# A head that centres tokens without a diagonal, and a fourth token tile that is loaded, normalised and transposed on its own

## The chip, the cores and the metric

The kernel runs on one core of one Trainium2 chip. The metric is the device time of one execution in microseconds; lower is better. The engines are named by what they do: TensorE (PE in the profile; its weight loads are PEld), VectorE (DVE), ScalarE (ACT), GpSimd (POOL) and SyncE (SP, which here only issues DMAs).

## What is computed

Two branches over the same layer-normalised input are added to the input itself. x is 2048 tokens by 512 features in bfloat16.

```python
xn = (x - mean(x)) / sqrt(var(x) + 1e-5)            # per token
# branch A: a diagonal complex state space model (S5)
Lam_bar = exp(exp(log_dt) * Lam)                    # 512 complex states
B_bar   = ((Lam_bar - 1) / Lam)[:, None] * (B_re + 1j * B_im)
Bu      = xn @ B_bar.T                              # 2048 x 512, complex
h[t]    = Lam_bar * h[t - 1] + Bu[t]                # scan over the 2048 tokens
y       = 2 * real(h @ C.T) + xn * Dskip
# branch B: SwiGLU, 512 -> 1376 -> 512
z = (silu(xn @ w_gate) * (xn @ w_up)) @ w_down
out = x + y + z
```

## The kernel before

The 2048 tokens are cut into four chunks of 512 (`CW`), and each chunk into four tiles of 128 tokens (`TPC`). The 1376 columns of `w_gate` and `w_up` are cut into three groups, `fgroups`: columns 0 to 511, 512 to 1023 and the rest. Loops are written out at build time, and the order of the instructions on every engine and queue is the order in which the code emits them (`manual_schedule`). Work of VectorE that isn't urgent is kept in a list, `backlog`, and emitted between TensorE's stages by `pump`, which counts off estimated microseconds; that order is fixed at build time too. Every TensorE result goes to a PSUM bank from a pool of eight (`bank()`), so that a new result waits until the tile eight before it has been read by ScalarE or VectorE.

**Loads.** SyncE issues the loads one after the other: x of tile 0, half of gate group 0 (L119), x of tile 2 (L132), both halves of up group 0, x of tile 3 (L135), gate and up of groups 1 and 2 (L114), and x of tiles 4 to 7 (L144). ScalarE's queue issues x of tile 1 and the other half of gate group 0.

**The head.** Most of the kernel needs the normalised input with features on the partitions. For chunk 0 that would take statistics, normalisation and a transpose before TensorE could begin. So the first three tiles (`SW` = 3) go another way: they are only centred (mean subtracted), transposed by TensorE against the identity (`cT_mm`, L242) and copied out of PSUM into `xcT` (`cT_copy`, L254); the factor 1/std of a token is put in later, as a scale of the ScalarE instruction that reads the gate or up result (`sw_gate` L500, `sw_out` L515).

For tiles 0 and 1 the mean is subtracted inside TensorE: `raw_mm` transposes the raw tile into PSUM, and `cT_mean` (L250) adds a product of the constant `minus_mean` (-1/512 everywhere) with `diag`, the identity scaled per token with the token's sum. The sum of tile 0 is a VectorE reduction (L219), that of tile 1 a ScalarE instruction (L222), and `diag` is built by VectorE (L229). For tile 2 the mean is a ScalarE instruction (`mean_act`, L225), the subtraction a VectorE instruction (`center`, L232), and TensorE transposes the centred tile. `head_mm` (L492, as all of `sw_mm`) then multiplies these tiles with group 0 of gate (which = 0) and up (which = 1), over four blocks k of 128 features each.

**Tile 3 and the rest of chunk 0.** `ln_stats` (L185, L186), `ln_rstd` (L194 on VectorE, the power -1/2 at L195 on GpSimd) and `norm_dve` (L203) normalise the four tiles into `xn_c[0]`, which shares its memory with the centred tiles, and one DMA transpose (`xT_dma`, L262) brings all four into `xnT[:, 0]`. Tile 3 of SwiGLU's first products and the state space projection of chunk 0 (`bproj_tile`, L384) read it. Behind it in SyncE's queue are the two transposing loads of the projection's weights `BT` (L148).

In between stand small steps for the state space model: `prm_transpose` (a TensorE product L278 and a VectorE copy L279), `exp_pool` (L282, a power on GpSimd), `pad_last` (three GpSimd memsets), an iota on GpSimd (L744), `params_a` (L285, L287), and `params_sin` (L323 to L339, two ScalarE sines). `table_ops` builds tables of sines from VectorE steps (L298 to L307) and ScalarE sines (L311).

**SwiGLU of chunk 0.** The remaining pairs of group and tile follow in this order, with L769 for the pairs of group 2, whose gate and up share one bank:

```python
for gi, i in [(1, 0), (1, 1), (1, 2), (2, 0), (2, 1), (2, 2), (0, 3), (1, 3), (2, 3)]:
```

The products of gate and up are VectorE instructions (L523). Then come the projection of chunk 0 (32 matmuls over eight banks), the last, narrow block of SwiGLU (`gateup_last`, L542, read by L544 and L545), the projection of chunk 1, and SwiGLU, scan, and output of the chunks in turn (L459, L426, L598, L611). The output is accumulated in memory: x is copied to the output by DMAs of 256 rows (`edges`, L857) and results are added by accumulating DMAs.

Of the kernel before, what the change touches and what calls it, by code (L numbers as in the profile page):

```python
# [10 lines left out]
F32 = mybir.dt.float32  # L11
# [12 lines left out]
def kernel(  # L24
# [52 lines left out]
    def flat(ap3):  # L77
        return ap3.rearrange("p q j -> p (q j)")
# [33 lines left out]
    def load_w1(q, tiles, view, gi):  # L112
        a, b = fgroups[gi]
        q.dma_start(out=tiles[gi][:, :, :], in_=view[:, :, a * 128:F if gi == len(fgroups) - 1 else b * 128])  # L114
# [9 lines left out]
    minus_mean = const.tile([128, 128], BF16, name="minus_mean")  # L124
    nc.sync.dma_start(out=xall[:, 0, :], in_=x_v[:, 0, :])
    nc.vector.memset(xall[:, 1, 0:2], 0.0)
    nc.vector.memset(minus_mean[:], -1.0 / D)
    nc.scalar.dma_start(out=xall[:, 1, :], in_=x_v[:, 1, :])
    nc.scalar.preload_act_table_set("silu_and_others")
    load_w1_half(nc.sync, wg_g, wg_v, 0, 0, HK)  # L130
# [1 line left out]
    nc.sync.dma_start(out=xall[:, 2, :], in_=x_v[:, 2, :])  # L132
    load_w1_half(nc.sync, wu_g, wu_v, 0, 0, HK)
    load_w1_half(nc.sync, wu_g, wu_v, 0, HK, KD)
    nc.sync.dma_start(out=xall[:, 3, :], in_=x_v[:, 3, :])  # L135
    load_w1(nc.sync, wg_g, wg_v, 1)
    load_w1(nc.sync, wu_g, wu_v, 1)
    load_w1(nc.sync, wg_g, wg_v, 2)
    load_w1(nc.sync, wu_g, wu_v, 2)
    prm_rows = const.tile([128, 128], BF16, name="prm_rows")  # L140
# [40 lines left out]
    def by_k(ap):  # L181
        return ap.rearrange("p (k d) -> p k d", d=128)

    def ln_stats(n):
        nc.vector.bn_stats(out=stats[:, n, 0, :], in_=xall[:, n, :])  # L185
        nc.vector.bn_aggr(out=mv[:, n, :], in_=stats[:, n, 0, :])  # L186
# [6 lines left out]
    def ln_rstd(a, b):  # L193
        nc.vector.tensor_scalar(out=ve[:, a:b], in0=mv[:, a:b, 1], scalar1=EPS, scalar2=None, op0=ALU.add)  # L194
        nc.gpsimd.tensor_tensor(out=rstd[:, a:b], in0=ve[:, a:b], in1=neg_half[:, 0:b - a], op=ALU.pow)  # L195
# [15 lines left out]


    xcT, xc = CF[:, 0], CF[:, 1]
    xn_c[0] = flat(xc).rearrange("p (k i d) -> p k i d", k=KD, i=TPC)
    sums = const.tile([128, 2], F32, name="sums")
    diag = const.tile([128, 2, 128], BF16, name="diag")

    def sum_dve(i):
        nc.vector.tensor_reduce(out=sums[:, i:i + 1], in_=xall[:, i, :], axis=mybir.AxisListType.X, op=ALU.add)  # L219

    def sum_act(i):
        nc.scalar.activation(out=xnT[:, NCH - 1, 0, :], in_=xall[:, i, :], func=ACT.Copy, accum_out=sums[:, i:i + 1])  # L222

    def mean_act(i):
        nc.scalar.activation(out=xnT[:, NCH - 1, 0, :], in_=xall[:, i, :], func=ACT.Copy, scale=1.0 / D,  # L225
                             accum_out=mean2[:])

    def diag_dve(i):
        nc.vector.tensor_scalar(out=diag[:, i, :], in0=ident[:], scalar1=sums[:, i:i + 1], scalar2=None, op0=ALU.mult)  # L229

    def center(i, mean):
        nc.vector.tensor_scalar(out=xc[:, i, :], in0=xall[:, i, :], scalar1=mean, scalar2=None, op0=ALU.subtract)  # L232

    mean2 = const.tile([128, 1], F32, name="mean2")
    p2, p0, p1 = bank(), bank(), bank()
    held = [[None, None] for _ in range(TPC)]
    held[0][0], held[1][0], held[0][1], held[1][1], held[2][0] = (bank() for _ in range(5))
    warm = held[1][0]
    raw = [[p0, p1, held[2][0], held[1][1]], [p2, p2, held[0][1], held[0][1]]]

    def cT_mm(ps, src, k, first, stop):
        nc.tensor.matmul(ps[:, k * 128:(k + 1) * 128], lhsT=src[:, k * 128:(k + 1) * 128], rhs=ident[:], start=first,  # L242
                         stop=stop)

    def raw_mm(i):
        for k in range(KD):
            cT_mm(raw[i][k], xall[:, i, :], k, k == 0 or raw[i][k] is not raw[i][k - 1], False)

    def cT_mean(i, k0, k1):
        nc.tensor.matmul(raw[i][k0][:, k0 * 128:k1 * 128], lhsT=minus_mean[:],  # L250
                         rhs=diag[:, i:i + 1, :].to_broadcast([128, k1 - k0, 128]), start=False, stop=True)

    def cT_copy(copy, ps, i, k0=0, k1=KD):
        copy(out=xcT[:, k0:k1, i * 128:(i + 1) * 128], in_=by_k(ps[:, k0 * 128:k1 * 128]))  # L254

    seen = const.tile([128, 1], BF16, name="seen")

    def runs(ap):
        return ap.rearrange("p k (i t) -> p (k i) t", t=128)

    def xT_dma(c):
        nc.sync.dma_start_transpose(out=runs(xnT[:, c]), in_=xn_tile(c)[:].rearrange("p k i d -> p (k i d)"))  # L262
# [13 lines left out]
    def prm_transpose():  # L276
        pp = p1[:, 0:128]
        nc.tensor.matmul(pp, lhsT=prm_rows[:], rhs=ident[:], start=True, stop=True)  # L278
        V.tensor_copy(out=prm[:].rearrange("p t q -> p (t q)"), in_=pp[:, 0:3 * NQ])  # L279

    def exp_pool(out, in_):
        nc.gpsimd.tensor_tensor(out=out, in0=e_t[:], in1=in_, op=ALU.pow)  # L282
# [96 lines left out]
    def bproj_tile(c, part, q):  # L379
        if c not in u_tiles:  # L380
            u_tiles[c] = ssm.tile([128, 2, NQ, CW], BF16, name="u16", bufs=2)
        ps = bank()
        for k in range(KD):
            nc.tensor.matmul(ps[:], lhsT=BT[:, part, k, q * 128:(q + 1) * 128], rhs=xnT[:, c, k, :],  # L384
                             start=(k == 0), stop=(k == KD - 1))
        nc.scalar.copy(out=u_tiles[c][:, part, q, :], in_=ps[:])  # L386

    def rotation(src, dst, back):
# [88 lines left out]
            g, u = guT[:fs, lo:fi + 1, :], u_pair[c][:fs, 0:fi - lo + 1, :]  # L477
            products.append(lambda: V.tensor_tensor(out=g, in0=g, in1=u, op=ALU.mult))  # L478

    SW = TPC - 1  # L480
    gu_tile(0)
    g0 = flat(gu_tile(1)[:]).rearrange("p (f i d) -> p f i d", f=FT, i=TPC)

    def tokens(i, k):
        if i < SW:
            return xcT[:, k, i * 128:(i + 1) * 128]
        return xnT[:, 0, k, i * 128:(i + 1) * 128]

    def sw_mm(ps, groups, gi, i, k0=0, k1=KD):
        a, b = fgroups[gi]  # L490
# [44 lines left out]
    def gateup_last(c):  # L535
        gl = g_last[c % 2][:] if c else g0[:, FT - 1]
        u = up_p.tile([128, TPC, FR], BF16, name="ul", bufs=2)
        for h in range(0, TPC, 2):
            ps = bank()[:, 0:4 * FR].rearrange("p (i w f) -> p i w f", i=2, w=2)
            for i in range(2):  # L540
                for k in range(KD):
                    nc.tensor.matmul(ps[:, i], lhsT=xnT[:, c, k, (h + i) * 128:(h + i + 1) * 128],  # L542
                                     rhs=w_end[:, k, :, FL - FE:FL - FE + FR], start=(k == 0), stop=(k == KD - 1))
            nc.scalar.activation(out=gl[:, h:h + 2, 0:FR], in_=ps[:, :, 0, :], func=ACT.Silu)  # L544
            nc.scalar.copy(out=u[:, h:h + 2, :], in_=ps[:, :, 1, :])  # L545

        def product():
            V.tensor_tensor(out=gl[:, :, 0:FR], in0=gl[:, :, 0:FR], in1=u[:], op=ALU.mult)
            if c:
                nc.sync.dma_start_transpose(out=gu_tile(c)[:, FT - 1:FT, :].rearrange("p f (i t) -> p (f i) t", t=128),  # L550
                                            in_=gl.rearrange("p i d -> p (i d)"))
            else:
                g0_dma(fgroups[1][1], FT)
        products.append(product)
# [111 lines left out]
    def dummy(ps, n, cols):  # L666
        for _ in range(n):
            nc.tensor.matmul(ps[:, 0:cols], lhsT=one.to_broadcast([128, 128]), rhs=one.to_broadcast([128, cols]),  # L668
                             start=True, stop=True)
# [22 lines left out]
    def head_mm(which, i, k0=0, k1=KD):  # L692
        if held[i][which] is None:
            held[i][which] = bank()
        sw_mm(held[i][which], (G, U)[which], 0, i, k0, k1)

    dummy(warm, 4, CW)
    dummy(warm, 5, 128)
    V.tensor_copy(out=seen[:], in_=ident[:, 0:1])
    sum_dve(0)  # L700
    sum_act(1)
    diag_dve(0)
    raw_mm(0)
    raw_mm(1)
    dummy(warm, 2, 128)
    for k in range(KD):
        cT_mean(0, k, k + 1)
    diag_dve(1)
    for k in range(KD):
        cT_copy(nc.scalar.copy if k % 2 else V.tensor_copy, raw[0][k], 0, k, k + 1)  # L710
    cT_mean(1, 0, HK)
    head_mm(0, 0, 0, 1)
    cT_mean(1, HK, KD)
    cT_copy(V.tensor_copy, raw[1][0], 1, 0, HK)
    cT_copy(nc.scalar.copy, raw[1][HK], 1, HK, KD)
    head_mm(0, 0, 1, HK)
    head_mm(0, 1, 0, HK)
    for k in range(HK, KD):
        for i in range(2):
            head_mm(0, i, k, k + 1)  # L720
    ln_stats(1)
    mean_act(2)
    ln_rstd(1, 2)
    ln_stats_half(0, 0)
    center(2, mean2[:])
    ln_stats_half(0, 1)
    ln_rstd(0, 1)
    for i in range(2):
        head_mm(1, i, 0, HK)
    for k in range(KD):  # L730
        cT_mm(p1, xc[:, 2, :], k, k == 0, k == KD - 1)
    cT_copy(nc.scalar.copy, p1, 2)
    for i in range(2):
        head_mm(1, i, HK, KD)
    ln_stats(3)
    ln_rstd(3, 4)
    ln_stats(2)
    ln_rstd(2, 3)
    head_mm(0, 2)
    sw_gate(0, 0, held[0][0])  # L740
    prm_transpose()
    exp_pool(dt_t[:], ldt)
    pad_last()
    nc.gpsimd.iota(out=jidx[:], pattern=[[1, CW]], base=0, channel_multiplier=0,  # L744
                   allow_small_or_imprecise_dtypes=True)
    sw_out(0, 0, None, held[0][1])
    head_mm(1, 2)
    for n in range(TPC):
        norm_dve(n)
    xT_dma(0)  # L750
    params_a()
    load_bt(0)
    load_bt(1)
    sw_out(0, 1, *held[1])
# [97 lines left out]
    gateup_chunk(1)  # L852
    nc.gpsimd.dma_start(out=dsk_bc[:], in_=A_Dskip.partition_broadcast(128))
    bproj_chunk(2)
    edges = [0, *range(HW, (NCH - 1) * CW + 1, HW)]
    for a, b in zip(edges, edges[1:]):
        nc.sync.dma_start(out=out[0, a:b, :], in_=A_x[0, a:b, :])  # L857
    queue_ssm(2)
# [47 lines left out]
```

## Time and profile before

| | us |
|---|---|
| median of 3 timed runs | 179.11 |
| the three runs | 178.34, 179.11, 179.14 |
| the profiled execution | 177.98 |
| its span | 175.8 |
| TensorE busy | 172.3 (98% of the span) |
| VectorE busy | 157.1 (89%) |
| ScalarE busy | 105.0 (60%) |
| GpSimd busy | 27.6 (16%) |
| granted TensorE clock | 1.00 |

The profile covers one execution, from the first instruction to the last; what lies around the span (2.2 us here) is start and end of the execution. All times inside the span count from its start. A row of the timeline gives start, busy time, engine, source line, operation and operands, the number of instructions merged into the row, and in brackets how long the engine was idle before and which event ended that. In rows of merged matmuls the time of one includes its pipeline, so that successive ones overlap. A DMA's issue is listed on its queue (SPq, ACTq) with the time of issuing; when the data is there is listed among the DMA issues, in microseconds from issue to landing.

### The profile page before, as it was taken

What the parts mean: (1) busy time and instruction counts of PE and PEld (TensorE: products, weight loads), DVE (VectorE), ACT (ScalarE), POOL (GpSimd) and SP (SyncE); (2) the same over time, 40 slices, a digit from 0 to 9 for tenths busy, and PEclk for the clock granted to TensorE, in tenths of its full rate; (3) what the DMA queues carried; (4) which work ended last, traced back from release to release, by engine and by line L of the source; (5) the groups of instructions that cost most, each with busy time, mean ns of one, the idle gap of its engine ahead of it and who ended that gap; (6) DMA issues with size and microseconds to landing.
All of it is one profiled execution on the core that took longest, in us unless ns stands there. A gap on an engine that the chain in (4) does not pass through costs nothing.

```text
span 175.8 us, 2386 instructions
## 1 busy us (share of the span) xinstructions
PE 172.3 (98%) x865; PEld 82.4 (47%) x865; DVE 157.1 (89%) x259; ACT 105.0 (60%) x191; POOL 27.6 (16%) x39
## 2 busy tenths in 40 slices
PE   8999999999999999999999999999999999999993
PEld 5444446464444444446444444446444444444542
DVE  3899989999999999999999999999999996799042
ACT  4579869798966687036996660024666658871000
POOL 5280300050000000046000000025000002507000
PEclk9999999999999999999999999999999999999999
DMA  5999979969999200036053000008310000994612
GB/s 165 338 352 185 204 147 243 209 97 231 246 207 300 108 4 0 0 36 83 2 64 89 0 0 0 0 4 79 40 30 2 0 4 5 164 186 43 80 62 62
DMA packets 35099, 17.88 MB, mean 102 GB/s; under 512 B 24880, under 2 KB 34960, under 8 KB 34992
## 3 DMA queue, kind: packets, MB, share of 16 engines
q1 hardware_dynamic: 31072, 13.96, 33.4%
q0 software_dynamic: 3456, 3.28, 15.0%
q10 hardware_dynamic: 560, 0.49, 0.9%
q8 instruction: 7, 0.11, 0.3%
q14 instruction: 4, 0.03, 0.1%
HBM read 8.03 MB, written 5.24 MB: 75 GB/s over the span
## 4 chain that ended last, share of the span: by engine, by line
PE 98%; DVE 0%; issue 0%
PE ps L459 29%; PE ps L598 22%; PE ps L611 16%; PE ps L384 16%; PE ps L492 8%; PE ps L542 3%; PE ps L769 2%; PE ps L668 1%; PE ps L242 1%; PE ps L250 0%; DVE xall L614 0%; PE ps L278 0%
## 5 line engine op out<-in xcount | busy, mean ns | idle before, releaser
L598 PE MATMUL ps<-wd_sb,guT 128*128 128x512 bf16 (+4 forms) x187 | 38.9, 366 | 0.0
L426 DVE TENSOR_TENSOR_SCAN g<-r_t,car,u 128x512 bf16<-128x512 f32 x24 | 29.0, 1263 | 0.0
L611 PE MATMUL ps<-CF,wt 128*128 128x512 bf16 (+2 forms) x136 | 28.5, 366 | 0.0
L384 PE MATMUL ps<-xnT,BT 128*128 128x512 bf16 x128 | 28.3, 379 | 0.0
L598 PEld LDWEIGHTS <-guT 128*128 128x128 bf16 (+1 forms) x187 | 17.9, 98 | 20.5
L459 PE MATMUL ps<-xnT,wg 128*128 128x512 bf16 x96 | 24.6, 379 | 0.0
L459 PE MATMUL ps<-xnT,wu 128*128 128x512 bf16 x96 | 24.6, 379 | 0.0
L618 POOL DMA_DIRECT2D out_dram<-res x12 | 10.5, 1044 | 81.6 <-ACT res L617 76.3
L473 ACT ACTIVATE guT<-ps 128x512 bf16<-128x512 f32 x30 | 18.0, 599 | 6.2 <-PE ps L459 5.8
L617 ACT CAST res<-ps 128x512 bf16<-128x512 f32 x12 | 7.0, 584 | 24.3 <-PE ps L611 24.3
L474 ACT CAST u<-ps 128x512 bf16<-128x512 f32 x30 | 17.6, 587 | 6.0 <-PE ps L459 5.9
L611 PEld LDWEIGHTS <-wt 128*128 128x128 bf16 x136 | 13.0, 98 | 14.7
L386 ACT CAST u<-ps 128x512 bf16<-128x512 f32 x32 | 17.6, 610 | 3.9 <-PE ps L384 3.9
L384 PEld LDWEIGHTS <-BT 128*128 128x128 bf16 x128 | 12.5, 98 | 14.9
L572 ACT ACTIVATE xr<-xall,nb,rstd 128x512 bf16<-128x512 bf16 x16 | 11.9, 805 | 5.5 <-DVE xall L580 2.7
L459 PEld LDWEIGHTS <-wu 128*128 128x128 bf16 x96 | 9.4, 98 | 11.3
L459 PEld LDWEIGHTS <-wg 128*128 128x128 bf16 x96 | 9.3, 98 | 10.6
L195 POOL TENSOR_TENSOR rstd<-ve,neg_half 128x1 f32<-128x1 f32 (+1 forms) x7 | 7.5, 1072 | 26.0 <-DVE ve L194 26.0
L459 PE MATMUL ps<-xnT,w_end 128*128 128x512 bf16 x48 | 10.8, 379 | 0.0
L185 DVE BATCH_NORM_STATS2 stats<-xall 128x6 f32<-128x512 bf16 x15 | 10.1, 671 | 0.4 <-DMA xall<-in_A_x_dram 0.3
L478 DVE TENSOR_TENSOR guT<-guT,u 128x1024 bf16<-128x1024 bf16 x15 | 10.1, 675 | 0.0
L394 DVE TENSOR_TENSOR pm<-u,c 128x2048 bf16<-128x2048 bf16 x8 | 9.8, 1222 | 0.1
(127 smaller groups left out, 211.6 us busy)
## 6 DMA issues: line engine op xcount, KB each, us to landing
out_dram<-in_A_x_dram SPq DMA_DIRECT2D x6, 256.0 KB, 4.9
out_dram<-res POOLq DMA_DIRECT2D x12, 128.0 KB, 3.2
out_dram<-xall POOLq DMA_DIRECT2D x3, 512.0 KB, 6.0
wd_sb<-in_B_w_down_dram SPq DMA_DIRECT2D x1, 1280.0 KB, 9.2
xall<-in_A_x_dram SPq DMA_DIRECT2D x1, 1024.0 KB, 7.0
wu<-in_B_w_up_dram SPq DMA_DIRECT2D x2, 256.0 KB, 4.6
wg<-in_B_w_gate_dram SPq DMA_DIRECT2D x1, 512.0 KB, 5.6
wu<-in_B_w_up_dram SPq DMA_DIRECT2D x1, 512.0 KB, 6.6
```

The lines of the kernel that those rows point to most:

```text
L185: nc.vector.bn_stats(out=stats[:, n, 0, :], in_=xall[:, n, :])
L384: nc.tensor.matmul(ps[:], lhsT=BT[:, part, k, q * 128:(q + 1) * 128], rhs=xnT[:, c, k, :], start=(k == 0), stop=(k == KD - 1))
L386: nc.scalar.copy(out=u_tiles[c][:, part, q, :], in_=ps[:])
L426: V.tensor_tensor_scan(out=g()[:, part, q, :], data0=r_t[:, q:q + 1].to_broadcast([128, CW]), data1=u_tiles[c][:, part, q, :], initial=ini ...
L459: nc.tensor.matmul(ps[:fs, lo:hi], lhsT=wslice(groups, fi, k), rhs=xnT[:, c, k, lo:hi], start=(k == 0), stop=(k == KD - 1))
L473: nc.scalar.activation(out=guT[:fs, fi, :], in_=psg[:fs], func=ACT.Silu)
L474: nc.scalar.copy(out=u_pair[c][:fs, fi % 2, :], in_=psu[:fs])
L492: nc.tensor.matmul(ps[:, 0:(b - a) * 128], lhsT=tokens(i, k), rhs=groups[gi][:, k, 0:(b - a) * 128], start=(k == 0), stop=(k == KD - 1))
L572: nc.scalar.activation(out=box["xr"][:], in_=xall[:, n, :], func=ACT.Identity, scale=rstd[:, n:n + 1], bias=nb[:, n:n + 1])
L598: nc.tensor.matmul(o[:], lhsT=gu_tiles[c][:fsz[fi], fi, i * 128:(i + 1) * 128], rhs=wd_sb[:fsz[fi], fi, lo:hi], start=(fi == 0), stop=False)
L611: nc.tensor.matmul(o[:], lhsT=w_tiles[c][:, part, q, i * 128:(i + 1) * 128], rhs=CF[:, part, q, lo:hi], start=False, stop=(part == 1 and q ...
L618: nc.gpsimd.dma_start(out=out_v[:, n, lo:hi], in_=res[:, lo:hi], accum_op=ALU.add)
```

## The change

- The sums of tiles 0 and 1 are both made by VectorE, by one instruction that adds the two halves of a token's features and accumulates the result over them, in bfloat16. `diag` is gone: `cT_mean` takes the sums, broadcast over 128 columns, as the stationary operand, and the identity scaled with -1/512 as the moving one. Two filler matmuls are dropped, and the order of copies and matmuls in the head is new.
- The mean of tile 2 is made by VectorE (the same kind of sum, and a scaling) instead of ScalarE.
- x of tile 3 is loaded behind gate and up of group 1 instead of ahead of them.
- Statistics and normalisation are emitted in another order: tile 2's statistics now stand behind `prm_transpose`, and those of tile 3 behind the normalisations of tiles 0 to 2. `exp_pool`, `pad_last` and the iota are ahead of tile 3's power on GpSimd, `params_a` ahead of its normalisation.
- Chunk 0 is kept with the tile as the outer index (`rows_first`), and its transpose is two DMAs: tile 3 first, then tiles 0 to 2.
- The first two output copies of 256 rows are one of 512 rows.

```diff
-    nc.vector.memset(minus_mean[:], -1.0 / D)
...
-    nc.sync.dma_start(out=xall[:, 3, :], in_=x_v[:, 3, :])
     load_w1(nc.sync, wg_g, wg_v, 1)
     load_w1(nc.sync, wu_g, wu_v, 1)
+    nc.sync.dma_start(out=xall[:, 3, :], in_=x_v[:, 3, :])
...
-    xn_c[0] = flat(xc).rearrange("p (k i d) -> p k i d", k=KD, i=TPC)
+    def rows_first(ap):
+        return flat(ap).rearrange("p (i k d) -> p k i d", k=KD, i=TPC)
+
+    xn_c[0], xnT0 = rows_first(xc), rows_first(xnT[:, 0])
+    sums = const.tile([128, 2], BF16, name="sums")
+    mean = const.tile([128, 2, 2], F32, name="mean")
+
+    def sum_dve(i, dst):
+        nc.vector.scalar_tensor_tensor(out=xnT[:, NCH - 1, i, 0:HW], in0=xall[:, i, 0:HW], scalar=1.0,
+                                       in1=xall[:, i, HW:D], op0=ALU.mult, op1=ALU.add, accum_out=dst)
+
+    def center(i):
+        total, m = mean[:, i - 2, 0:1], mean[:, i - 2, 1:2]
+        sum_dve(i, total)
+        nc.vector.tensor_scalar(out=m, in0=total, scalar1=1.0 / D, scalar2=None, op0=ALU.mult)
+        nc.vector.tensor_scalar(out=xc[:, i, :], in0=xall[:, i, :], scalar1=m, scalar2=None, op0=ALU.subtract)
...
-    raw = [[p0, p1, held[2][0], held[1][1]], [p2, p2, held[0][1], held[0][1]]]
+    raw = [[p0, p1, held[2][0], held[1][1]], [p2, held[0][1], p2, held[0][1]]]
...
+    def cT_mean(i, *ks):
+        nc.tensor.matmul(by_k(raw[i][ks[0]][:])[:, ks[0]:ks[-1] + 1:HK], lhsT=sums[:, i:i + 1].to_broadcast([128, 128]),
+                         rhs=minus_mean[:, None, :].to_broadcast([128, len(ks), 128]), start=False, stop=True)
+
+    def raw_copy(i, k):
+        cT_copy(V.tensor_copy if k % 2 else nc.scalar.copy, raw[i][k], i, k, k + 1)
...
+    def xT0_dma(i0, i1):
+        nc.sync.dma_start_transpose(out=flat(xnT[:, 0])[:, i0 * D:i1 * D].rearrange("p (n t) -> p n t", t=128),
+                                    in_=flat(xc)[:, i0 * D:i1 * D])
...
-            nc.tensor.matmul(ps[:], lhsT=BT[:, part, k, q * 128:(q + 1) * 128], rhs=xnT[:, c, k, :],
-                             start=(k == 0), stop=(k == KD - 1))
+            nc.tensor.matmul(ps[:] if c else by_k(ps[:]), lhsT=BT[:, part, k, q * 128:(q + 1) * 128],
+                             rhs=xnT[:, c, k, :] if c else xnT0[:, k], start=(k == 0), stop=(k == KD - 1))
...
     dummy(warm, 4, CW)
     dummy(warm, 5, 128)
-    V.tensor_copy(out=seen[:], in_=ident[:, 0:1])
-    sum_dve(0)
-    sum_act(1)
-    diag_dve(0)
+    nc.vector.tensor_scalar(out=minus_mean[:], in0=ident[:], scalar1=-1.0 / D, scalar2=None, op0=ALU.mult)
+    for i in range(2):
+        sum_dve(i, sums[:, i:i + 1])
     raw_mm(0)
+    for k in range(HK):
+        cT_mean(0, k)
+        raw_copy(0, k)
     raw_mm(1)
-    dummy(warm, 2, 128)
-    for k in range(KD):
-        cT_mean(0, k, k + 1)
-    diag_dve(1)
-    for k in range(KD):
-        cT_copy(nc.scalar.copy if k % 2 else V.tensor_copy, raw[0][k], 0, k, k + 1)
-    cT_mean(1, 0, HK)
-    head_mm(0, 0, 0, 1)
-    cT_mean(1, HK, KD)
-    cT_copy(V.tensor_copy, raw[1][0], 1, 0, HK)
-    cT_copy(nc.scalar.copy, raw[1][HK], 1, HK, KD)
-    head_mm(0, 0, 1, HK)
-    head_mm(0, 1, 0, HK)
+    for k in range(HK, KD):
+        cT_mean(0, k)
+    for k in range(HK):
+        cT_mean(1, k, k + HK)
+        raw_copy(1, k)
+    for i in range(2):
+        head_mm(0, i, 0, HK)
+        for k in range(HK, KD):
+            raw_copy(i, k)
     for k in range(HK, KD):
         for i in range(2):
             head_mm(0, i, k, k + 1)
-    ln_stats(1)
-    mean_act(2)
-    ln_rstd(1, 2)
     ln_stats_half(0, 0)
-    center(2, mean2[:])
+    center(2)
     ln_stats_half(0, 1)
     ln_rstd(0, 1)
-    for i in range(2):
-        head_mm(1, i, 0, HK)
+    ln_stats(1)
+    ln_rstd(1, 2)
+    for k in range(HK):
+        for i in range(2):
+            head_mm(1, i, k, k + 1)
     for k in range(KD):
         cT_mm(p1, xc[:, 2, :], k, k == 0, k == KD - 1)
     cT_copy(nc.scalar.copy, p1, 2)
-    for i in range(2):
-        head_mm(1, i, HK, KD)
-    ln_stats(3)
-    ln_rstd(3, 4)
-    ln_stats(2)
-    ln_rstd(2, 3)
+    for k in range(HK, KD):
+        for i in range(2):
+            head_mm(1, i, k, k + 1)
     head_mm(0, 2)
     sw_gate(0, 0, held[0][0])
     prm_transpose()
+    ln_stats(2)
+    ln_rstd(2, 3)
     exp_pool(dt_t[:], ldt)
     pad_last()
     nc.gpsimd.iota(...)
     sw_out(0, 0, None, held[0][1])
     head_mm(1, 2)
-    for n in range(TPC):
+    for n in range(SW):
         norm_dve(n)
-    xT_dma(0)
+    ln_stats(SW)
+    ln_rstd(SW, TPC)
     params_a()
+    norm_dve(SW)
+    xT0_dma(SW, TPC)
+    xT0_dma(0, SW)
     load_bt(0)
     load_bt(1)
     sw_out(0, 1, *held[1])
...
-    edges = [0, *range(HW, (NCH - 1) * CW + 1, HW)]
+    edges = [0, *range(2 * HW, (NCH - 1) * CW + 1, HW)]
```

More of the change, by code (lines that the diff above doesn't have):

```diff
@@ L213 @@
     xcT, xc = CF[:, 0], CF[:, 1]
-    xn_c[0] = flat(xc).rearrange("p (k i d) -> p k i d", k=KD, i=TPC)
[L215 to L234, printed above, removed]
+    SW = TPC - 1
+    def rows_first(ap):
[11 more added lines that the diff above has]
+        nc.vector.tensor_scalar(out=xc[:, i, :], in0=xall[:, i, :], scalar1=m, scalar2=None, op0=ALU.subtract)
     p2, p0, p1 = bank(), bank(), bank()
@@ L246, in raw_mm @@
         for k in range(KD):
[L247 to L251, printed above, removed]
+            cT_mm(raw[i][k], xall[:, i, :], k, all(p is not raw[i][k] for p in raw[i][:k]), False)
+    def cT_mean(i, *ks):
[3 more added lines that the diff above has]
+        cT_copy(V.tensor_copy if k % 2 else nc.scalar.copy, raw[i][k], i, k, k + 1)
     def cT_copy(copy, ps, i, k0=0, k1=KD):
         copy(out=xcT[:, k0:k1, i * 128:(i + 1) * 128], in_=by_k(ps[:, k0 * 128:k1 * 128]))
-    seen = const.tile([128, 1], BF16, name="seen")
     def runs(ap):
         return ap.rearrange("p k (i t) -> p (k i) t", t=128)
+    def xT0_dma(i0, i1):
+        nc.sync.dma_start_transpose(out=flat(xnT[:, 0])[:, i0 * D:i1 * D].rearrange("p (n t) -> p n t", t=128),
+                                    in_=flat(xc)[:, i0 * D:i1 * D])
     def xT_dma(c):
@@ L478, in gu_out @@
             products.append(lambda: V.tensor_tensor(out=g, in0=g, in1=u, op=ALU.mult))
-    SW = TPC - 1
     gu_tile(0)
@@ L486, in tokens @@
             return xcT[:, k, i * 128:(i + 1) * 128]
-        return xnT[:, 0, k, i * 128:(i + 1) * 128]
+        return xnT0[:, k, i, :]
     def sw_mm(ps, groups, gi, i, k0=0, k1=KD):
@@ L541, in gateup_last @@
                 for k in range(KD):
-                    nc.tensor.matmul(ps[:, i], lhsT=xnT[:, c, k, (h + i) * 128:(h + i + 1) * 128],
+                    nc.tensor.matmul(ps[:, i],
+                                     lhsT=xnT[:, c, k, (h + i) * 128:(h + i + 1) * 128] if c else xnT0[:, k, h + i, :],
                                      rhs=w_end[:, k, :, FL - FE:FL - FE + FR], start=(k == 0), stop=(k == KD - 1))
```

## The prediction

> **What bounds the kernel now.** I read the page first, for the engine that carries the end.
>
> ```profile
> span 175.8 us, 2386 instructions
> ...
> PE 98%; DVE 0%; issue 0%
> ```
>
> The chain that ended last is TensorE almost alone: only a TensorE wait that goes, or a new one, moves the end. So I looked for waits in the chain in order of time (start, length, what).
>
> ```profile
> 4.72 0.39 PE ps L492
> 5.11 0.11 PE ps L250
> 5.22 2.49 PE ps L492 x11
> ```
>
> From 5.22 on the chain is matmuls back to back. One of 128x512 starts 0.216 us after the last (the 32 of L384 start within 7.07 - 0.38 = 6.69 us: 6.69 / 31). Eleven are 2.38, and the piece has 2.49: a gap of 0.11 us, the last in the kernel. In the timeline the matmul behind it starts at 5.82. What comes in then is a load: start, issue time and queue are in the timeline, the time to landing in the list of DMA issues (last number).
>
> ```profile
> 1.35 0.42 ACTq L119 DMA_DIRECT2D wg<-in_B_w_gate_dram  x1
> 2.16 0.94 SPq L119 DMA_DIRECT2D wu<-in_B_w_up_dram  x2
> ```
>
> ```profile
> wu<-in_B_w_up_dram SPq DMA_DIRECT2D x2, 256.0 KB, 4.6
> wg<-in_B_w_gate_dram ACTq DMA_DIRECT2D x1, 256.0 KB, 4.4
> ```
>
> The second half of gate group 0 lands at 1.35 + 4.4 = 5.75 to 5.8, just ahead of the matmul at 5.82 that needs it. The first up half (4.5 for that issue alone) lands at 2.16 + 4.5 = 6.66, and its first matmul starts at 6.68. So the head already runs at the pace of its weights.
>
> Next I read the timeline of VectorE, GpSimd, ScalarE and SyncE where tile 3 is normalised.
>
> ```profile
> 9.02 0.55 POOL L195 TENSOR_TENSOR rstd<-ve,neg_half 128x1 f32<-128x1 f32 x1 [0.82 <-DVE ve L194]
> 9.87 0.17 DVE L279 COPY prm<-ps 128x12 f32<-128x12 f32 x1
> 10.02 0.70 POOL L195 TENSOR_TENSOR rstd<-ve,neg_half 128x1 f32<-128x1 f32 x1 [0.45 <-DVE ve L194]
> 10.54 1.02 POOL L282 TENSOR_TENSOR dt_t<-e_t,prm 128x4 f32<-128x4 f32 x1
> 11.52 3.09 SPq L262 DMA_TRANSPOSE xnT<-CF  x1
> 11.82 0.68 DVE L523 TENSOR_TENSOR guT<-guT,u 128x1024 bf16<-128x1024 bf16 x1
> 11.96 0.56 POOL L744 IOTA jidx<- 128x512 f32 x1
> 13.63 0.67 ACT L500 ACTIVATE guT<-ps,rstd 128x512 bf16<-128x512 f32 x1
> ```
>
> From 11.82 to 24.9 VectorE has no listed idle time: whatever comes late at 11.82 is as late at 24.9. There ScalarE waits for it, and TensorE's banks hang on ScalarE:
>
> ```profile
> 22.50 7.07 PE L384 MATMUL ps<-xnT,BT 128*128 128x512 bf16 x32
> 24.94 1.06 ACT L311 ACTIVATE c<-pm 128x1024 bf16<-128x1024 f32 x1 [1.55 <-DVE pm L307]
> 26.17 0.38 ACT L515 ACTIVATE u<-ps 128x256 bf16<-128x256 f32 x1
> 30.73 7.07 PE L384 MATMUL ps<-xnT,BT 128*128 128x512 bf16 x32
> 32.53 1.06 ACT L311 ACTIVATE c<-pm 128x1024 bf16<-128x1024 f32 x1 [1.16 <-DVE pm L307]
> 33.71 0.31 ACT L545 CAST ul<-ps 128x192 bf16<-128x192 f32 x1
> ```
>
> **Part 1, the head.** It removes two diag builds (0.57 us of L229 on VectorE), two ScalarE sums (0.63 + 0.19 each) and two filler matmuls (0.106 each). A sum becomes a VectorE instruction over 256 pairs; no row shows that form. Nearest are 0.42 (statistics of 256) and 0.69 (the sum of 512); I take 0.43, both reading 256 positions. Sums from 3.07 and 3.43, first mean matmul at 3.6, copies (0.28 each, two engines) until 5.5, first gate matmul near 4.66 instead of 4.72, its first four done by 5.5. Then the second gate half is awaited, as now, until 5.8; four matmuls end at 6.68, and the up half lands at 6.66. Gain: at most the 0.02 us that the up half leaves, at worst nothing; I take 0. If the sums cost 0.69, the copies end 0.5 us later, and the first four matmuls take the place of the gap: a loss of up to 0.3 us, kept for the range.
>
> **Part 2, centring tile 2** goes to VectorE: a sum 0.43, a scaling 0.15, the subtraction 0.34 as now. From 5.46: half statistics, then the sum from 5.79 (x of tile 2 lands at 1.65 + 3.8 = 5.45), the subtraction at about 6.46, against 6.45 now. TensorE transposes tile 2 at 7.55, so up to 0.5 us is hidden. Cost 0.
>
> **Part 3, x of tile 3** goes behind group 1's weights in SyncE's queue. The four loads concerned carry the same bytes, so it lands when the second of those weights does now, 4.14 + 6.6 = 10.74, instead of 7.85. Group 1's weights come about 0.4 us earlier, worth nothing: gate 1 lands at 9.26 and is used at 10.42.
>
> **Part 4, VectorE's order behind the head.** The parameter copy (L279) now stands ahead of the statistics of tile 2. It waits for TensorE's parameter matmul, whose place in TensorE's order is unchanged: it starts at 9.50 and takes 0.22, so the copy starts at 9.77. VectorE is through with tile 1 at about 8.6 and waits 1.2 us, with statistics, normalisations, and all that follows, queued behind. From there, by the spacing of the rows (statistics of a tile, three instructions: 1.02; a normalisation: 0.33):
> - statistics of tile 2 from 9.85, its variance at 10.79; GpSimd's power starts 0.23 later (8.79 to 9.02), 11.02, and takes 0.55 to 0.70;
> - normalisations 0, 1 under it, 2 at 11.62 to 11.76; statistics of tile 3 until about 13.0 (its x landed at 10.74: hidden by 1.2 us);
> - GpSimd's queue: the power of dt 0.52 behind the start of the last (10.02 to 10.54), 11.54; then three memsets and iota, which starts 1.42 later (10.54 to 11.96), 12.96; the next 0.53 behind (a power follows iota at 12.49), so tile 3's power is at 13.49, not at 13.2 when its variance is there, and ends at 14.04 to 14.19;
> - normalisation of tile 3 at 14.08 to 14.23, the product of L523 two instructions on at 14.48 to 14.63.
>
> Now that product starts at 11.82: VectorE is 2.66 to 2.81 us later. At 14.39 it now waits for x of tiles 4 to 7, some 0.1 to 0.2 us, which is absorbed. Lateness at 24.9: 2.5 to 2.7.
>
> **What it costs TensorE.** ScalarE's first wait behind is the sine of the parameters (13.03 now); gate (1,0) moves from 13.63 to about 16.4. There are eight PSUM banks, so a tile waits until the one eight before it has been read.
> - Tile (2,2), from 17.32, needs gate (1,0), read by 17.1: 0.2 us to spare.
> - The eighth projection tile starts at 22.50 + 28 x 0.216 = 28.54 and needs the bank of (2,3), read at 26.17 + 0.38 = 26.55. That read stands behind the sine that waits for VectorE, so it goes with the lateness. Less 0.05 from read to matmul, cover is 1.94; stall 0.56 to 0.76.
> - The seventh of the next 32 starts at 30.73 + 24 x 0.216 = 35.91 and needs the bank read by 33.71 + 0.31 = 34.02, also behind such a sine: cover 1.84, stall 0.66 to 0.86 in all (not added: the first shifts both).
> Further on TensorE is 0.8 late, VectorE 2.6: 1.8 apart. The output coefficients are done at 70.4 and used from 72.64, cover 2.2. Nothing more is added.
>
> **Part 5, the transposes.** Tile 3's is issued at about 14.6. A 128x512 one (guT from g_last) lands in 2.4 us: 17.0, needed by the weight load at 17.97. The other three tiles go 1.2 us behind; four tiles take 3.7 (xnT from xn), so they land by 19.5; both BT loads follow, now landing 1.9 and 2.3 us apart: 21.4 and 23.7, for 22.3 and 25.9. Hidden, with 0.9 us of cover at its thinnest. The moving operand in runs of 128 is 0.216 by the nearest row (L769, runs of 256); taken as free. The merged store is the same bytes.
>
> **Sum.** Head 0, tile 3 at the middle of 0.66 to 0.86: +0.76 us. The profiled execution took 177.98 us (span 175.8 and 2.2 around): 178.7 after. It lies 1.13 under the median of 179.11; on the median, 179.9.
>
> **The rivals.**
> *Transposes late.* If the tile-3 power or x slips by over 0.9 us, TensorE waits at 17.97 or 22.3 instead. For it: the whole chain of part 4 is in one row, and x is fourth in a queue whose engines are full until 14.4. Against: the loads ahead are the same bytes. At 2 us of slip: 1.1 us there, and ScalarE's stall grows to 2.8: 181.9; at 1 us, 180.9.
>
> *GpSimd held up by VectorE.* Tile 2's power now runs beside normalisations 0 and 1; beside normalisations it took 0.70 in the row at 10.02, beside statistics 0.55. Should it wait for both (0.66 more, its start at 11.52), tile 3's power is 0.5 later: stall 1.26, 180.4. The Trainium skill ("SBUF — State Buffer", Who interferes with whom) says that GpSimd and a VectorE tensor_scalar in a two-port mode take one port pair by exclusive lock. The rows show 0.15, not a full block.
>
> *The lateness is absorbed.* Were the three normalisations ahead or GpSimd's queue quicker by 0.7 us, the stall ends: 179.1. Against it: each term is a row.
>
> *Faster.* The timed runs are up to 1.16 us above the profiled one. The transpose of four tiles lands at 11.52 + 6.1 = 17.6, 0.35 ahead of its use; if in those runs it comes some 1.1 late, tile 3's own transpose, with 0.9 of cover, takes the wait away: 178.0, from the point where ScalarE's lateness is also under 1.8. For it: loads fill the queue until 14.4. Against: the profiled execution has no wait there to remove.
>
> **How the numbers follow.** Forecast 0.54: 179.5 to 180.4, its middle close under the bound of no change, so 0.28 below and 0.26 above it. Transposes late 0.12, GpSimd held 0.07, both slower. Absorbed 0.13, all within. Faster 0.14: 0.10 by over 0.5%, 0.04 within. Half a percent, 0.9 us, is about what a measurement of this kernel can tell from no change: 178.2 and 180.0. Faster 0.10, same 0.45, slower 0.45. The range leaves out most of the faster case and the far end of the late transposes, some 0.1 each: 178.3 to 181.2; the forecast alone spans 179.5 to 180.4.
>
> **What would show it.** Right: the first group-0 gate matmul behind the gap still at 5.8, VectorE idle some 1.2 us before L279's copy, the tile-3 transpose issued near 14.6, the product of L523 near 14.55, and TensorE idle about 0.6 near 28.5 and 0.1 near 36, in the projection. Wrong: gate matmuls past 5.8 without a gap or the up half landing before 6.3 (a gain in the head), VectorE not waiting at the copy, or a TensorE wait at 18 or 22.

## The result and the profile after

| | before | changed |
|---|---|---|
| median of 22 runs each, us | 178.39 | 179.59 |
| profiled execution, us | 177.98 | 179.66 |
| its span, us | 175.8 | 177.6 |

The changed kernel is slower: ratio 1.0065, 95% interval 1.0051 to 1.0080, which is 1.2 us. The ratios here, and those of the experiments, leave disturbed runs out.

The page shows that TensorE no longer carries the end alone; DMA has 7% of the chain.

```profile
span 177.6 us, 2365 instructions
...
PE 85%; DMA 7%; POOL 2%; DVE 2%; issue 1%; SPq 1%; ACT 1%
```

The chain in order of time (start, length, what) names two transfers, the first load of BT and the transpose of chunk 2. Each is followed by matmuls that TensorE could have begun earlier.

```profile
17.60 5.96 DMA BT<-in_A_B_re_dram
23.61 7.08 PE ps L385 x32
...
53.45 4.49 DMA xnT<-xn
57.99 5.14 PE ps L385 x23
```

The timeline of TensorE shows how long it stood still. The first projection matmul starts at 23.61 (22.50 before), 1.03 us later than back to back; that of chunk 2 at 57.99 (56.22 before), another 0.65 later by the starts of the matmuls, of which the row shows 0.49.

```profile
23.61 7.08 PE L385 MATMUL ps<-xnT,BT 128*128 128x512 bf16 x32 [0.86 <-DMA BT<-in_A_B_re_dram]
57.99 2.33 PE L385 MATMUL ps<-xnT,BT 128*128 128x512 bf16 x10 [0.49 <-DMA xnT<-xn]
```

With 0.08 us in the head that is 0.08 + 1.03 + 0.65 = 1.76 us, the difference of the two first matmuls of chunk 2 (57.99 - 56.22) and of the spans (1.8). The two profiled executions differ by 1.68 us, 0.5 us more than the medians.

Where the lateness comes from is in the timeline of VectorE, GpSimd and SyncE:

```profile
9.90 0.17 DVE L280 COPY prm<-ps 128x12 f32<-128x12 f32 x1 [0.96 <-ACT u L515]
11.15 0.65 POOL L194 TENSOR_TENSOR rstd<-ve,neg_half 128x1 f32<-128x1 f32 x1 [1.57 <-DVE ve L193]
13.19 0.56 POOL L742 IOTA jidx<- 128x512 f32 x1
13.71 0.54 POOL L194 TENSOR_TENSOR rstd<-ve,neg_half 128x1 f32<-128x1 f32 x1
14.29 0.41 DVE L202 TENSOR_SCALAR CF<-xall,mv,rstd 128x512 bf16<-128x512 bf16 x1 [0.90 <-POOL rstd L194]
14.69 0.68 DVE L523 TENSOR_TENSOR guT<-guT,u 128x1024 bf16<-128x1024 bf16 x1
14.73 2.83 SPq L259 DMA_TRANSPOSE xnT<-CF  x2
```

VectorE idles 0.96 us ahead of the parameter copy (the bracket names ScalarE; the copy reads TensorE's matmul, which started at 9.57), tile 3's power waits for iota, the normalisation 0.90 us for the power. The product of L523 stands at 14.69 for 11.82, the first transpose at 14.73 for 11.52.

### The profile page after: what moved, and what is told of

It is laid out like the page before. It is cut to its first block, busy times and chain, and to the rows that moved or that the text cites. A ratio compares the mean times of both kernels' runs of the same rounds, so it can differ in the third digit from the quotient of the medians.

```text
span 177.6 us, 2365 instructions
## 1 busy us (share of the span) xinstructions
PE 171.8 (97%) x847; PEld 82.4 (46%) x863; DVE 157.2 (89%) x263; ACT 102.4 (58%) x188; POOL 28.0 (16%) x39
## 3 DMA queue, kind: packets, MB, share of 16 engines
HBM read 8.03 MB, written 5.24 MB: 75 GB/s over the span
## 4 chain that ended last, share of the span: by engine, by line
PE 85%; DMA 7%; POOL 2%; DVE 2%; issue 1%; SPq 1%; ACT 1%
PE ps L460 27%; PE ps L599 21%; PE ps L385 16%; PE ps L612 16%; DMA BT<-in_A_B_re_dram 3%; PE ps L542 3%; DMA xnT<-xn 3%; PE ps L492 1%; DMA xall<-in_A_x_dram 1%; SPq L259 1%; PE ps L238 1%; POOL rstd L194 1%; POOL dt_t L283 1%; PE ps L246 1%; ACT u L515 0%
## 5 line engine op out<-in xcount | busy, mean ns | idle before, releaser
L599 PEld LDWEIGHTS <-guT 128*128 128x128 bf16 (+1 forms) x187 | 17.9, 98 | 20.5
L460 PE MATMUL ps<-xnT,wg 128*128 128x512 bf16 x91 | 23.9, 379 | 0.1
L475 ACT CAST u<-ps 128x512 bf16<-128x512 f32 x30 | 17.9, 595 | 5.1 <-PE ps L460 5.1
L612 PEld LDWEIGHTS <-wt 128*128 128x128 bf16 x136 | 13.0, 98 | 14.7
```

Source lines behind the costliest of these rows:

```text
L460: nc.tensor.matmul(ps[:fs, lo:hi], lhsT=wslice(groups, fi, k), rhs=xnT[:, c, k, lo:hi], start=(k == 0), stop=(k == KD - 1))
L475: nc.scalar.copy(out=u_pair[c][:fs, fi % 2, :], in_=psu[:fs])
L599: nc.tensor.matmul(o[:], lhsT=gu_tiles[c][:fsz[fi], fi, i * 128:(i + 1) * 128], rhs=wd_sb[:fsz[fi], fi, lo:hi], start=(fi == 0), stop=False)
L612: nc.tensor.matmul(o[:], lhsT=w_tiles[c][:, part, q, i * 128:(i + 1) * 128], rhs=CF[:, part, q, lo:hi], start=False, stop=(part == 1 and q ...
```

## Experiments

Four theories were set against one another. *Lateness*: the new order makes tile 3 late, and SyncE's queue and VectorE with it. *Late load*: tile 3's x does that. *Split*: the second DMA transpose is the cost. *Head*: the new head is. The bank wait of the prediction is a fifth.

### Tile 2's statistics ahead of the parameter copy

```diff
+    ln_stats(2)
+    ln_rstd(2, 3)
     prm_transpose()
-    ln_stats(2)
-    ln_rstd(2, 3)
```

> The changed kernel with one edit: statistics and power of tile 2 stand ahead of the parameter copy again. Lateness theory (tile 3 is normalised 2.5 us and more later because VectorE waits at the parameter copy with both tiles' statistics behind it; everything that SyncE and VectorE do afterwards is late by that): VectorE spends its 1.0 us of idle time before the copy on tile 2, tile 3's transpose is issued about 1.2 us earlier (13.5 for 14.73), the first BT load lands at about 22.4 for 23.56 and TensorE's wait of 1.0 us there goes; the transpose of chunk 2 lands 1.2 us earlier, which leaves about 0.4 us of wait near 57. Ratio to before about 1.0025 (0.9995 to 1.004). Late-load theory (tile 3's x, landing at 10.9, sets the time): the transpose doesn't move, ratio 1.0065. Split theory (the second DMA transpose is what is slow): the wait at BT shrinks by no more than the earlier issue, but the three tiles still take 5.6 us from issue to landing. Head theory (the new head costs it): nothing moves but by 0.1 us, ratio 1.0065.

Ratio 1.0001 (0.9985 to 1.0016): the whole loss is gone with two lines moved. The SyncE and VectorE rows of this kernel:

```profile
10.33 0.17 DVE L280 COPY prm<-ps 128x12 f32<-128x12 f32 x1
13.75 2.83 SPq L259 DMA_TRANSPOSE xnT<-CF  x2
```

VectorE comes to the copy without listed idle time, and the transpose is issued 1.0 us earlier than in the changed kernel. The first BT load lands 6.0 us behind its issue at 16.62, at 22.6, and TensorE does not wait for it. For chunk 2's transpose it still waits 0.16 us by the starts of the matmuls (about 0.4 expected). This execution's head was 0.4 us late. Late load, head and split fall as causes by themselves: all three are still in this kernel, and the second transpose still takes 5.6 us.

### x of tile 3 loaded early

```diff
+    nc.sync.dma_start(out=xall[:, 3, :], in_=x_v[:, 3, :])
     load_w1(nc.sync, wg_g, wg_v, 1)
     load_w1(nc.sync, wu_g, wu_v, 1)
-    nc.sync.dma_start(out=xall[:, 3, :], in_=x_v[:, 3, :])
```

> The changed kernel with x of tile 3 loaded where it was before, ahead of group 1's weights. Lateness theory: x of tile 3 lands near 7.8 for 10.9, but VectorE comes to it at 12.2 in either case, so the transpose is issued at 14.7 as in the changed kernel and the ratio stays at 1.0065 (1.005 to 1.008). Late-load theory: ratio back to 1.000, transpose issued up to 3 us earlier. Split and head theories: as the changed kernel.

Ratio 1.0046 (1.0028 to 1.0065). The transpose is issued at 14.58, and TensorE waits for BT as before the edit (1.19 us by the starts of the matmuls). For chunk 2's transpose, issued 0.8 us earlier than in the changed kernel's profile, it does not wait here, so that second wait is not in every execution. The ratio lies a little under the expected 1.005 to 1.008; its interval overlaps that of the changed kernel, so whether the place of the load is worth 0.1% stays open. It is not the cause.

### One transpose instead of two

```diff
-    xT0_dma(SW, TPC)
-    xT0_dma(0, SW)
+    xT0_dma(0, TPC)
```

> The changed kernel with one DMA transpose for all four tiles of chunk 0, issued at about 14.7. Split theory (two DMAs cost 1 us more of the DMA engines' time than one): the four tiles land 3.7 us behind the issue, near 18.4, the first BT load near 20.4 instead of 23.56; TensorE waits 0.3 to 0.6 us near 18.2 for the four tiles and not at BT. The later wait for chunk 2's transpose near 57 stays, about 1 us, so the ratio is 1.004 to 1.007. Lateness theory, in which splitting is free: the four tiles land when the second DMA did, 21.7, TensorE waits for tile 3 some 3.5 us near 18, ratio about 1.018, and the first BT load lands at 23.5 as before.

Ratio 1.0171 (1.0134 to 1.0209), as the lateness theory had it. The head of this execution was 0.9 us late, so the transpose is issued at 15.61 for the expected 14.7. The four tiles land 5.9 us behind it, and TensorE waits for tile 3, 2.45 us by the starts of the matmuls (3.5 expected):

```profile
21.59 1.04 PE L492 MATMUL ps<-wg,xnT 128*128 128x512 bf16 x4 [2.29 <-DMA xnT<-CF]
```

Splitting costs nothing that one transpose would save. It protects: with the same late order, tile 3 alone is there in time, and the loss is 0.65% instead of 1.7%.

### The first BT load ahead of the transposes

```diff
+    load_bt(0)
     norm_dve(SW)
     xT0_dma(SW, TPC)
     xT0_dma(0, SW)
-    load_bt(0)
     load_bt(1)
```

> The changed kernel with the first BT load emitted ahead of the two transposes of chunk 0, so that SyncE issues it near 8.2 while VectorE is still on tile 3. It takes the wait for BT away and leaves VectorE's lateness as it is. Bank theory (that of the prediction): with BT there, the projection starts at 22.6, and TensorE waits 0.55 to 0.75 us near 28.6 for the bank of gate and up (2,3), and 0.1 near 36; then again for chunk 2's transpose near 57 (0.5 to 0.9), which lands as late as in the changed kernel. Ratio 1.0055 to 1.0075, since the last of these waits sets the sum. Split theory: the three tiles alone take 5.6 us from issue; they land near 21.7 and are there in time. If BT alone were the loss: no other wait appears, ratio 1.000 to 1.002.

Ratio 1.0074 (1.0053 to 1.0094). The wait for BT is gone, and the bank wait that the prediction priced is there in its place. ScalarE's and TensorE's rows of this kernel:

```profile
28.34 1.06 ACT L312 ACTIVATE c<-pm 128x1024 bf16<-128x1024 f32 x1 [2.46 <-DVE pm L308]
29.57 0.38 ACT L515 ACTIVATE u<-ps 128x256 bf16<-128x256 f32 x1
30.00 1.02 PE L385 MATMUL ps<-xnT,BT 128*128 128x512 bf16 x4 [0.48 <-ACT u L515]
```

The bank of pair (2,3) is read at 29.57 + 0.38 = 29.95, the eighth projection tile starts at 30.00, and back to back it would have started 0.64 us earlier (the starts of the matmuls; the row shows 0.48). Expected were 0.55 to 0.75 at this place. The head of this execution was 0.8 us late, which shifts all of it. The transpose of chunk 2 is waited for again, 0.37 by the starts and 0.21 in its row (expected 0.5 to 0.9). Removing one of the waits in a row buys nothing as long as another ends as late.

### The head alone

```diff
     # kernel before, with
-    sum_dve(0); sum_act(1); diag_dve(0)
+    sum_dve(0, sums[:, 0:1]); sum_dve(1, sums[:, 1:2])
     ...           # new cT_mean, raw_copy, center and their order; no filler matmuls behind raw_mm(1)
```

> The kernel before with the new head alone (VectorE sums, no diagonal, no filler matmuls, centring of tile 2 on VectorE); x of tile 3, the order behind the head, the layout and the single transpose as before. Weights theory (the head runs at the pace of gate group 0's second half and up group 0's first half): ratio 1.000 (0.998 to 1.002); the four gate matmuls behind the second gate half start as that lands, 5.7 to 6.0. Clock theory (new, from runs in which 512-column matmuls start 0.427 us apart until 5.2 to 6.8 us instead of 0.216: without the fillers TensorE is still at half speed when the head's real work comes): some executions lose 0.3 to 0.9 us, ratio 1.002 to 1.004. A head that is shorter as built would be 0.997 to 0.998.

Ratio 0.9998 (0.9984 to 1.0012). The new head costs nothing and brings nothing. The loss that the clock theory had is not in the median.

### Both BT loads ahead of the transposes

```diff
+    load_bt(0)
+    load_bt(1)
     norm_dve(SW)
     xT0_dma(SW, TPC)
     xT0_dma(0, SW)
-    load_bt(0)
-    load_bt(1)
```

> The changed kernel with both BT loads emitted ahead of the two transposes of chunk 0, so that nothing transposing follows these in the queue. Interleaving theory (the second transpose takes 5.6 us from issue to landing because the BT loads behind it share the DMA engines' transposing): it lands 3 to 3.6 us behind its issue. Own-length theory (three tiles of this transpose take 4.4 us whatever follows): still 5.5 to 5.9 us. In both, tile 3's transpose comes behind two BT loads, lands near 18.5 to 20 and TensorE waits for it 0.5 to 2 us near 18.2, so the ratio is 1.006 to 1.015 and tells nothing between them.

Ratio 1.0146 (1.0093 to 1.0199), in the expected range and telling nothing, as said there. The landings: the second transpose is there 5.2 us behind its issue in the list of DMA issues, which neither theory had; the BT loads are ahead of it in the queue. Counted from the landing of tile 3's transpose ahead of it, the three tiles take 2.7 us here (20.2 to 22.9), and 4.4 in the changed kernel (17.25 to 21.67) and with one BT load behind them (17.9 to 22.3). That alone would speak for interleaving with the transposing loads behind. But two later kernels with both BT loads behind have short distances too: with fillers the three tiles land 2.0 us behind tile 3 (18.20 to 20.17), with head and split alone 3.2 (15.08 to 18.30). There tile 3's own transpose took 4.5 and 3.9 us, so this distance decides nothing. From issue to landing it is 5.1 to 5.7 us in all eight kernels that split. What makes it so long is open.

### GpSimd's memsets and iota behind tile 3's power

```diff
     # first experiment, and
-    pad_last()
-    nc.gpsimd.iota(...)
     sw_out(0, 0, None, held[0][1])
     ...
     ln_rstd(SW, TPC)
+    pad_last()
+    nc.gpsimd.iota(...)
     params_a()
```

> The kernel of the first run of this study (tile 2's statistics ahead of the parameter copy), with GpSimd's three memsets and iota emitted behind tile 3's power as well. Lateness theory: tile 3's power starts about 0.5 us earlier than there, its transpose is issued near 13.2, chunk 2's transpose lands another 0.5 us earlier and its wait near 57 (0.17 to 0.5 us there) goes. Ratio 0.998 to 1.000. If what remains in that run is the head's, nothing moves: 1.000.

Ratio 0.9999 (0.9981 to 1.0017), no different from the first experiment. Tile 3's power starts at 12.83, but its execution's group-0 loads landed up to 0.7 us later than in the changed kernel's, VectorE waited 0.20 us for tile 3's x (landed at 11.62), and the transpose was issued at 13.85, not 13.2. Nothing was left to gain, or too little to measure.

### The same with filler matmuls

```diff
     # experiment before, and
-    dummy(warm, 5, 128)
+    dummy(warm, 8, 128)
     ...
     raw_mm(1)
+    dummy(warm, 2, 128)
```

> The kernel before in this list with five filler matmuls more (three more at the start, and the two that the change dropped). Clock theory: TensorE reaches full speed by about 4.5 us as in the kernel before, and executions in which 512-column matmuls start 0.427 us apart behind 5 us are rare; ratio 0.997 to 0.999, 0.1 to 0.3 us faster than the kernel without them. Weights theory: the head waits for its weights in any case, ratio the same as without them within 0.001.

Ratio 0.9985 (0.9959 to 1.0010): not distinguishable from the kernel before, nor from the one without fillers. The expected full speed by 4.5 us did not come: in the profiled execution the 512-column matmul at 5.21 is followed by the next at 5.64.

### The order alone, in the kernel before

```diff
-    ln_stats(3)
-    ln_rstd(3, 4)
-    ln_stats(2)
-    ln_rstd(2, 3)
     head_mm(0, 2)
     sw_gate(0, 0, held[0][0])
     prm_transpose()
+    ln_stats(2)
+    ln_rstd(2, 3)
     ...           # dt power, memsets, iota
-    for n in range(TPC):
+    for n in range(SW):
         norm_dve(n)
-    xT_dma(0)
+    ln_stats(SW)
+    ln_rstd(SW, TPC)
     params_a()
+    norm_dve(SW)
+    xT_dma(0)
```

> The kernel before with the new order alone: tile 2's statistics behind the parameter copy, tile 3's behind the normalisations of tiles 0 to 2, GpSimd's dt power, memsets and iota ahead of tile 3's power. Head, load of tile 3, layout and the single transpose are those of before. Lateness theory: the one transpose is issued near 14.7 (11.52 before) and lands some 6 us behind; TensorE waits 2 to 3 us near 18.2 for tile 3; ratio 1.014 to 1.019, as for the changed kernel with one transpose (1.0171). If the loss of the changed kernel needed the new head or the late load, this is near 1.000.

Ratio 1.0100 (1.0077 to 1.0124). The order makes the kernel slower by itself, with the old head, the early load and the single transpose. Its rows:

```profile
9.96 0.17 DVE L279 COPY prm<-ps 128x12 f32<-128x12 f32 x1 [2.14 <-ACT u L515]
14.79 2.01 SPq L262 DMA_TRANSPOSE xnT<-CF  x1
20.28 1.04 PE L492 MATMUL ps<-wg,xnT 128*128 128x512 bf16 x4 [1.80 <-DMA xnT<-CF]
```

The issue is where it was expected. The size was missed (1.014 to 1.019 expected): the transpose landed 5.4 us behind it, not 6, and TensorE waited 1.96 us by the starts of the matmuls instead of 2 to 3. It is the only wait behind the head: chunk 2's transpose, issued at 53.24, lands in 3.7 us and is in time.

### The head and the split, without the order

```diff
     # changed kernel, with
+    nc.sync.dma_start(out=xall[:, 3, :], in_=x_v[:, 3, :])   # ahead of group 1
     ...
+    ln_stats(3); ln_rstd(3, 4); ln_stats(2); ln_rstd(2, 3)    # ahead of head_mm(0, 2)
     ...
+    norm_dve(SW)
+    xT0_dma(SW, TPC)
     for n in range(SW):
         norm_dve(n)
+    xT0_dma(0, SW)
     params_a()
     ...           # the same lines are gone from their later places
```

> The new head and the split transpose with everything else as before: x of tile 3 loaded early, its statistics, power and normalisation first, its transpose issued ahead of the normalisations of tiles 0 to 2. Lateness theory: tile 3's transpose is issued near 10.5 to 11.5, the rest and both BT loads are in the queue by then, nothing waits behind the head; ratio 0.998 to 1.001, no faster than before, since TensorE's matmuls from 6.7 us on are the same and were back to back. Split theory: the BT load lands near or behind its use at 22.5 and TensorE waits there; ratio 1.003 or more.

Ratio 0.9987 (0.9971 to 1.0003). The two parts without the order do no harm. This is the best candidate of the study, and it isn't shown to beat the kernel before. Its timeline shows why a shorter head brings nothing:

```profile
4.41 1.02 PE L492 MATMUL ps<-wg,CF 128*128 128x512 bf16 x4
6.19 1.02 PE L492 MATMUL ps<-wg,CF 128*128 128x512 bf16 x4 [0.76 <-DMA wg<-in_B_w_gate_dram]
```

The first gate matmuls start 0.3 us earlier than in the kernel before (4.72), and TensorE then waits 0.76 us for the second gate half.

## Why the prediction was right, and where it was not

**The number.** Forecast were +0.76 us and 179.9, within 178.3 to 181.2; measured +1.2 us and 179.59. The 22 runs of before have a lower median (178.39) than the three shown (179.11), so that the absolute number is so near is luck. In part the difference is too: the 0.76 us was the price of a wait for a PSUM bank that did not occur, and two waits for transfers that the sum had at nothing came in its place. The half percent was passed: of the cases it is the slower one, at 0.45.

**Part 1, the head: right in its price, not in its course.** The sums took 0.42 and 0.43 us (0.43 forecast), and 0.09 for reading the accumulator, which was not foreseen. The head alone is 0.9998. But in the profile of the changed kernel the first gate matmul starts at 5.00 (4.66 forecast), the second gate half is there at 5.24, and the eight gate matmuls pass 5.8 without a gap, one of the prediction's signs of being wrong. The first up matmul comes at 6.76 all the same (6.68 before), 0.3 us behind its weights. The wait for the weights is in other executions: 0.76 us with head and split alone.

**Parts 2 and 3: right.** Centring tile 2 is hidden, and x of tile 3 landed at 10.9 (10.74 forecast), ahead of its reader at 12.2.

**Part 4, the order: right, to within 0.3 us in every term.** VectorE's idle time was 0.96 (1.2 forecast), the copy at 9.90 (9.77), tile 3's power at 13.71 (13.49), the product at 14.69 (14.48 to 14.63), the transpose at 14.73 (14.6). ScalarE's sine that waits for VectorE came at 27.61, 2.67 late (2.5 to 2.7 forecast). The first experiment shows that the loss needs this lateness, and *the order alone* that the lateness is enough for a loss.

**The bank wait: right in size, but not what ended last.** It is in the trace as soon as BT is there in time: 0.64 us for 0.56 to 0.76. In the changed kernel TensorE already stood still 1.03 us for BT; it came to this bank that much later, and the bank had been read.

**Part 5, the transposes: wrong.** This is the step that failed. The three tiles were to land 3.7 us behind their issue, at 19.5, by the row for the transposes of the later chunks (3.7 for four tiles). The list of DMA issues of the changed kernel, for the first transpose alone and for the second alone (last number: from issue to landing):

```profile
xnT<-CF SPq DMA_TRANSPOSE x1, 2.5
xnT<-CF SPq DMA_TRANSPOSE x1, 5.6
```

Tile 3's 2.4 was right; the other three took 5.6 and landed at 21.67. The nearer row was chunk 0's own, 6.1, which the prediction used only for its faster case. Loads ahead of it in the queue do not explain that row: with none left (the DMA engines moved nothing in the microsecond ahead of the issue), the one transpose of the third experiment still took 5.9. The first BT load landed 1.9 us behind the three tiles, as forecast, but at 23.56 instead of 21.4, and the cover of 0.9 us became a wait of 1.03. That it can go this way was the rival *transposes late*, at 0.12, which tied it to a slip of tile 3's power or x; the slip was in the second transpose.

**"Nothing more is added": wrong.** Only VectorE's lateness was carried forward, not that of SyncE's queue. Chunk 2's transpose was issued at 53.45 for 50.44 and cost the second wait. The queue's lateness is not all of that wait. Issue and first matmul of before, then from the pages of before and after the median of the three later chunks' transposes, from issue to landing:

```profile
50.44 1.60 SPq L262 DMA_TRANSPOSE xnT<-xn  x1
56.22 7.07 PE L384 MATMUL ps<-xnT,BT 128*128 128x512 bf16 x32
```

```profile
xnT<-xn SPq DMA_TRANSPOSE x3, 3.7
xnT<-xn SPq DMA_TRANSPOSE x3, 4.5
```

At 3.7 us it would have landed at 57.15, ahead of the 57.34 at which TensorE would have come to it. Chunk 1's and chunk 2's take 3.6 to 3.7 us in both kernels with the old head (before, and the order alone) and 4.3 to 4.6 in all ten with the new one. Why is open; no run separates it. By itself it costs nothing: the head alone has it too.

**The other rivals.** GpSimd was not held up: the power beside the normalisations took 0.65 us, between its two rows of before. The Trainium skill ("SBUF — State Buffer", Who interferes with whom) would have it wait for a whole VectorE instruction in a two-port mode; this trace shows 0.1 us over the power beside statistics. Whether the normalisations run in such a mode is not shown. The lateness was not absorbed. No gain over the kernel before appeared from tile 3 coming first; with the late order it saves what the third experiment lost.

## What to carry to other kernels

An engine that executes in order pays for a wait with everything queued behind it: two lines moved behind a copy that waits for TensorE cost 1 us of VectorE, and without that move the loss is gone. Price a transfer by the row of that same transfer, not by one of its size elsewhere in the kernel, and follow the lateness of a queue to each of its later entries, not only the next. Of waits in a row, a later one adds only what goes beyond the lateness that is there already: the bank wait of 0.64 us added nothing behind the 1.03 for BT, and came back when that was taken out.

## What was not expected of the hardware

**TensorE's start at half speed.** Back to back, 512-column matmuls start 0.216 us apart, but in the first microseconds 0.427. When that ends differs between executions: in the profile of before ahead of 4.2 us, in the changed kernel at about 5.2, and with the first BT load first only at about 6.8, where eight gate matmuls took 2.87 us (1.89 in the first experiment):

```profile
4.79 2.87 PE L492 MATMUL ps<-wg,CF 128*128 128x512 bf16 x8
```

The granted clock reads 1.00 in the same stretch, so it doesn't show this. The Trainium skill ("TensorE: Matmul & The Clock Gate", What's actually happening) says that the array runs at half rate until about 3.4 us of sustained work, in a free-running window, so that the count of slow matmuls varies from run to run. The traces agree on the half rate and on the variation, but not on one time: TensorE begins at 0.78, isn't busy all the time, and the speed changes between about 3.7 (head and split) and 6.9 (both BT loads first), which is 2.9 to 6.1 us later. Whether fillers can shorten this is open: five of them made no measurable difference.

**Transposes of one size and different lengths.** A DMA transpose of chunk 0's four tiles took 5.4 to 6.1 us from issue to landing in the four kernels that have it, whether loads stood ahead of it (6.1 in the kernel before) or none (5.9 in the third experiment). That of chunk 1 or 2, of the same size, took 3.6 to 4.6. In all of the four, the transposing loads of BT stand behind chunk 0's and a plain load or copy behind the others; that this is the reason is not shown, since three tiles took 5.2 us also with nothing transposing behind them.
